# One batch of a two-level Strassen down projection taken back to one level in three of its seven products, with the weight sums made later

## The chip, the cores and the metric

The kernel runs on one core of one Trainium2 chip. The metric is device microseconds for one execution: 713.79 us is the median of three runs before the change (713.74 to 713.90). The profile is of one execution, whose own time was 713.74 us.

## The reference

Two blocks follow each other. The first is a cross attention between 512 tokens and 32 states, for 8 batches of 8 heads of 64 features, read in both directions. The second is a two-layer network with a gelu of the form h * sigmoid(1.702 h).

```
scores  = x @ state^T / 8       ; a  = exp(scores  - max) / (sum + 1e-9) ; xread = a  @ state   (512 rows per batch)
scores2 = state @ x^T / 8       ; a2 = exp(scores2 - max) / (sum + 1e-9) ; sread = a2 @ x       (32 rows per batch)
rows = [xread, sread] per batch, heads side by side -> 4352 rows of 512
h = rows @ w_in (512 x 2048) ;  g = h / (1 + exp(-1.702 h)) ;  out = g @ w_out (2048 x 512)
```

All is float32, except that the weights arrive as 64-bit floats and are rounded in the kernel.

## The kernel before, in words

**Order of the work.** The order is written out by hand: each engine executes its instructions in the order in which the program issues them, and a wait holds up all that stands behind it on that engine. TensorE works batch by batch. Batch 0 goes through a plain up projection (`up_x`) and a plain down projection (`down`, a loop over `f` = 0 to 15), during which the weights `w_out` still arrive and are rounded on VectorE, and during which batch 1's up projection runs too. From batch 1 on, each pass of the loop `for b in range(1, B)` (line 1268) is one down projection, `strassen_two` with `key` = b, followed by the up projection of batch b + 1. While the down projection of batch b runs, the attention of batch b + 1 is slipped in through *hooks*: `hooks_next` (line 901) makes a table from a place's name to a list of steps, and `hook(name)` issues them there. The 256 rows of `sread` come last.

**Strassen.** In `strassen_two` w_out has the quarters B11, B12, B21, B22, each 1024 x 256, and the gelu output has quarters of 1024 features x 256 tokens. The seven products of Strassen's method (Winograd's form) are issued as P1, P2, P5, P6, P3, P7, P4. Their right factors are B11, B21, T1 = B12 - B11, T2 = B22 - T1, B22, T3 = B22 - B12 (in the place of B12), T4 = B21 - T2. P1 and P2 are issued as *plain* products: `product` (line 742), in two halves, after each of which comes a hook (P1a, P1b and so on). Each half is 8 matmuls of 128 x 128 by 256 columns; the profile shows each of these float32 matmuls as two instructions, so 16 for a half. P5, P6, P3, P7 and P4 are issued as *low* products: `strassen_low` (line 687) uses the same method once more inside, with seven products of 4 matmuls by 128 columns (8 instructions each), small VectorE additions between them (line 701), ScalarE copies (lines 705, 711), and a hook after each (P5.1 to P5.7).

**Sums.** A low product needs three sums of blocks of its right factor (`low_sums`: three VectorE subtractions of 128 x 512, line 1210) and a fourth made in place (`low_third`). It also needs three sums and one in place of its left factor (line 752). The right factors are the same for all batches, so their sums are made once and kept in DRAM (`low_keep`, line 648). They are loaded back into two rooms `low_a` and `low_b` by `low_load` (line 645) in three parts; those of T4 go to a third room. Before the change, the sums for B22, T1, T3 and T2 are made at the end of batch 0's down loop, and those for T4 in the hook `run` of batch 1.

**Attention of the next batch, inside `strassen_two`.** The scores of batch b + 1 come at hook P2a. VectorE transposes them into `e1` (line 351) and takes maxima (lines 358, 416); ScalarE takes exponentials. The exponentials of the states' direction go out to DRAM and come back as 32 x 32 blocks (`eT_out` line 468, `eT_in` line 476), and VectorE turns each block in place (`eT_turn`, line 480). Then TensorE computes `att_sread` (line 500), which needs the turned exponentials, and two `att_M` (line 320). In every batch before the change these three stand in the hook `run`, between P3 and P7. `x_sum`, `x_inverse`, `x_scale` and `x_back` (lines 431 to 447) normalise the other direction.

**Steps the change touches.** `steps3`, `steps4` and `steps12` are the left sums for P7, P4 and P3 (four pairs of 128 x 256 each). `sums_of` and `third_of` make those of S1 (for P5) and S2 (for P6). `s4` subtracts S2 from A12 in four steps. `low4_make` makes and keeps the T4 sums in batch 1. `s12` and `s3` make S1, S2, S3. The last ones of batch 1 (line 1262) stand ahead of `strassen_two` on VectorE.

Of the kernel before, what the change touches and what calls it, by code (L numbers as in the profile page):

```python
# [10 lines left out]
FP32 = mybir.dt.float32  # L11
# [9 lines left out]
def kernel(  # L21
# [32 lines left out]
    B, H, S, D = x.shape  # L54
# [602 lines left out]
    def low4_make(a):  # L657
        t = low4_room()
        for fn, args in low_sums(T4, low_parts(t)):
            fn(*args)  # L660
        low_keep(4, t)
        a["low4"] = t

    def low4_load(a):
        a["low4"] = low4_room()
# [2 lines left out]
    def spare_M():  # L668

        m = [mpool.tile([P, NG, FC], FP32, tag=f"M{i}", name="spare_M") for i in (2, 3)]  # L670
        return [v[:, g] for v in m for g in range(NG)]
# [53 lines left out]

    def strassen_two(key, dst, hooks, a4):

        B11, B21, B22 = w_out[:, :HF, :HN], w_out[:, HF:, :HN], w_out[:, HF:, HN:]
        g = [G[key, u] for u in range(HF)]
        half = S // 2  # L730
# [45 lines left out]
        def sums_of(*pairs):  # L776
            for s, (r1, r2, r4) in pairs:
                tt(r1, whole(s, 1, 0), whole(s, 1, 1))
            for s, (r1, r2, r4) in pairs:
                tt(r2, r1, whole(s, 0, 0), ALU.subtract)  # L780
            for s, (r1, r2, r4) in pairs:
                tt(r4, whole(s, 0, 1), r2, ALU.subtract)
# [7 lines left out]

        product(bank(0), A_of(0, 0), B11, "P1")
        nc.scalar.copy(k1, bank(0))
        *r, p5 = spare_M()
        r = [v.rearrange("p (k h t) -> p k h t", k=2, h=2) for v in r]
        p5 = p5.rearrange("p (r n) -> p r n", r=2)
        sums_of((S1, r), (S2, (q1, q2, q4)))
        third_of(S1)
        product(bank(1), A_of(0, 1), B21, "P2")
        osb = opool.tile([P, 2, HN], FP32, tag="osb", name=f"osb_{key}_00")
        tt(osb, bank(1), k1)  # L800
# [6 lines left out]
        hook("P2")  # L807
        first = [lambda: s4(0), lambda: s4(1), lambda: third_of(S2), lambda: s4(2), lambda: s4(3)]
        o, h0, h1 = low_banks()

        def at(i):
            for fn in first[i - 1 : i]:
                fn()
            hook(f"P5.{i}")

        b11, t3, b21, b22 = halves_of(T1)
        strassen_low(left_of(S1, *r), (b11, t3, b21, b22, *low_b), [h0, h1, o], p5, at)
        low_load(6, 1)
        hook("P5")
        o, h0, h1 = low_banks()  # L820
        banks = [h0, o, h1]

        def sums(y, rooms):

# [31 lines left out]

        steps3, left3 = sums(y_of(0, half), (v1, v2, v4))
        steps4, left4 = sums(y_of(NU, half), (q1, q2, q4))
        steps12, left12 = sums(y_of(NU, 0), r)
        own6 = {2: steps12[:1], 5: steps12[1:2]}  # L860
        lowly("P6", left_of(S2, q1, q2, q4), T2, low_a, banks, k2, own6)
        low_load(3, 0)
        tt(k2, k2, k1)
        tt(t01, p5, k2)
        hook("P6")
        p3 = o01
        o, h0, h1 = low_banks()
        own3 = {1: steps12[2:3], 2: steps12[3:]}
        if key + 1 == B:

            own3.update({i + 3: steps3[i : i + 1] for i in range(4)})
        lowly("P3", left12, B22, low_b, [h0, h1, o], p3, own3)
        if key + 1 < B:
            low_load(5, 1)
        hook("run")
        if key + 1 < B:
            for fn in steps3:
                fn()
        hook("T")
        o, h0, h1 = low_banks()  # L880
        lowly("P7", left3, T3, low_a, [o, h0, h1], k3, {k + 1: steps4[k : k + 1] for k in range(4)})
        if key + 1 < B:
            low_load(2, 0)
        osb = opool.tile([P, 2, HN], FP32, tag="osb", name=f"osb_{key}_11")
        then = [
            lambda: tt(osb, k3, t01),
# [2 lines left out]
            lambda: tt(o01, p3, t01),  # L889
            lambda: out(0, 1, o01),  # L890
        ]
        o, h0, h1 = low_banks()
        lowly(
            "P4", left4, T4, low_parts(a4["low4"]), [o, h1, h0], k1, {2: then[:2], 3: then[2:3], 4: then[3:]}
        )
        p4 = k1
        tt(o10, p4, k3)
        out(1, 0, o10)
        free.extend(g)
# [1 line left out]
    def hooks_next(b):  # L901

        h = {}

        def at(name, fn, *args):
            h.setdefault(name, []).append((fn, args))

        at("P1a", att_state, b)
        at("P2a", att_scores, b)

        at("P2a", load_x, b)
        at("P2a", att_M, b, 0)
        at("P2a", att_M, b, 1, True)
        at("P2a", att_blocks, b)
        at("P2a", att_s_max, b)
        at("P2a", att_s_exp, b)
        at("P2a", eT_out, b)
        at("P2a", x_max, b, 0)
        at("P2a", x_sub, b, 0)
        at("P5.1", x_exp, b, 0)  # L920
        at("P5.6", att_s_norm, b)
        at("P5.6", x_max, b, 1)
        at("P5.7", x_sub, b, 1)
        at("P6.1", x_exp, b, 1)
        steps = up_sums(b)

        A[b]["sums"] = {0: steps[9:11], 1: [steps[11], steps[14]]}
        attention = [
            ("P6.1", x_sum, 0), ("P6.3", x_sum, 1), ("P6.3", x_inverse), ("P6.4", x_scale, 0),
        ]  # L930
        attention += [
            ("P6.6", x_scale, 1), ("P3.3", x_back, 0), ("P3.4", x_back, 1), ("P3.5", eT_turn, 0), ("P3.6", eT_turn, 1),
            ("P5", eT_in), ("run", att_sread), ("run", att_M, 3, True), ("run", att_M, 2),
        ]
        names = {"T": range(5), "P7.5": (5, 6), "P7.6": (7,), "P4.1": (8,), "P4.5": (12, 13)}
        for name, fn, *args in attention:
            at(name, fn, b, *args)
        for name, n in names.items():
            for i in n:
                at(name, steps[i][0], *steps[i][1])  # L940
        at("P7.2", att_srT, b)
        return h


# [264 lines left out]
    def T_of(t, x0, x1):  # L1209
        nc.vector.tensor_tensor(out=t, in0=x0, in1=x1, op=ALU.subtract)  # L1210

    def low_made(k, t, i):

        for fn, args in low_sums(t, (low_a, low_b)[i]):
            fn(*args)
        low_keep(k, turn_rooms[i])

    def low_away(k, t):

        room = apool.tile([P, NPR, S], FP32, tag="xT", name=f"away_{k}").rearrange("p j t -> p (j t)")[:, : 3 * FC]  # L1220
        for fn, args in low_sums(t, low_parts(room)):
            fn(*args)
        low_keep(k, room)


    rest = list(range(2 * nper, NF))
    for f in range(NF):
        rounds(1)
        round_to(NFC * NPR + f + 1)
        for r in range(SCH):  # L1230
            down(0, r, [f], out_x[0, r], r == SCH - 1)
        if f in (0, 2):
            for g in range(NG):
                att_eT(f // 2, g)
        if f in (0, nper * 2):
            att_M(1, 2 + f // (nper * 2))
        if f in (1, 3):
            att_sread(f // 2)
        if f in (2, 4):
            att_srT(f // 2 - 1)  # L1240
        if f % 2 == 1:
            up_x(1, rest.pop(0))
        if f == HF:
            load_state(2)
            load_x_squares(2)
        if f == NF - 2:
            T_of(T1, B12, B11)
            low_away(6, B22)
            low_made(5, T1, 1)
            for u in range(NU - 1):  # L1250
                s12(1, u, S)
            T_of(T2, B22, T1)
            low_third(T1)
        if f == NF - 1:
            for u in range(NU - 1):
                s3(1, u, S)
            T_of(B12, B22, B12)
            low_away(3, T3)
            low_third(T3)
            turn_x(2)  # L1260
            low_made(2, T2, 0)
    s12(1, NU - 1, S)
    s3(1, NU - 1, S)

# [3 lines left out]
    for b in range(1, B):  # L1268
        if b > 1:
            ahead = {"P1a": [(up_strassen(b, S, *parts_x(b), A[b]["sums"]), ())]}  # L1270
        else:
            ahead = {"P1a": [(low_third, (B22,)), (T_of, (T4, B21, T2)), (low_third, (T2,))], "P7.7": [(low_third, (T4,))]}
        if b + 1 < B:
            if b > 1:
                turn_x(b + 1)
            hooks = hooks_next(b + 1)
        else:

            steps, left, right = sr_sums()
            order = (  # L1280
                ("P5.6", 2), ("P6.1", 3), ("P6.3", 6), ("P6.4", 7), ("P7.5", 8), ("P7.6", 9), ("P4.1", 16, 17), ("P4.5", 18, 19),
            )
            hooks = {name: [steps[i] for i in n] for name, *n in order}
            hooks["P3.7"] = [(low_third, (T1,))]
            beside = steps[10:16] + [(low_third, (t,)) for t in (T2, T3, T4, B22)]
            ahead["P1a"][:0] = [steps[i] for i in (0, 1, 4, 5)]
        for name, first in ahead.items():
            hooks[name] = first + hooks.get(name, [])
        a4 = {}

        at = hooks.setdefault("run", [])
        k = 3 if b + 1 < B else 0
        at[k:k] = [(low4_load if b > 1 else low4_make, (a4,))]
        strassen_two(b, out_of(b), hooks, a4)
        if b + 2 < B:
            load_state(b + 2)
            load_x_squares(b + 2)
# [35 lines left out]
```

## Time and profile before

| what | value |
|---|---|
| median of three runs | 713.79 us |
| profiled execution, its own time / span | 713.74 / 712.0 us |
| TensorE busy | 697.9 us (98%) |
| VectorE busy | 602.0 us (85%) |
| ScalarE busy | 231.2 us (32%) |
| stretch from 154.85 to 232.04 (down of batch 1, up of batch 2) | 77.19 us |
| the five like it after it (batches 2 to 6) | 75.62 or 75.63 us each |
| granted TensorE clock, whole span | 0.998 |

A line of the timeline has the start, the length, the engine, the line of the kernel, the operation, what it writes and reads, the shapes, a count, and in brackets how long the engine was idle before it and what ended that. Matmuls overlap their successors, so the time that one takes from TensorE is read as the difference between the starts of two groups, not from the lengths.

### The profile page before, as it was taken

The page shows a single profiled execution, that of the slowest core. Times are in us where ns is not written, and L with a number is a line of the kernel's source. Part 1 is how long each engine was busy: PE and PEld are TensorE (multiplying, and loading weights), DVE is VectorE, ACT ScalarE, POOL GpSimd, SP SyncE. Part 2 cuts the span into 40 slices and gives each one's busy share as a digit, 9 for nine tenths or more (in the row PEclk, how much of TensorE's full clock was granted, in tenths as well). Part 3 has the DMA queues.
Part 4 walks back from the last instruction along what each step waited for, and adds up shares of the span by engine and source line. Part 5 has one row for each costly group of instructions (what it writes and reads, how often), then busy time and mean ns, then how long its engine had stood idle before and what let it go on. Part 6 is the DMA issues. An engine that isn't in the chain of part 4 may idle for free.

```text
span 712.0 us, 12663 instructions
## 1 busy us (share of the span) xinstructions
PE 697.9 (98%) x4973; PEld 557.9 (78%) x4975; DVE 602.0 (85%) x1246; ACT 231.2 (32%) x456; POOL 0.8 (0%) x8
## 2 busy tenths in 40 slices
PE   8989999999999999999999999999999999999996
PEld 3433444457888799888998899879987998899995
DVE  6999899969988999789968997899789997888650
ACT  5686511023214322433233322441343224300210
POOL 0000000000000000000000000000000000000000
PEclk9999999999999999999999999999999999999999
DMA  8921246217633184408550674138431940031001
GB/s 234 363 78 53 95 150 138 115 45 188 190 128 61 34 202 144 87 0 182 164 118 1 117 202 119 29 71 192 141 60 34 203 145 22 0 114 66 16 1 29
DMA packets 143770, 77.10 MB, mean 108 GB/s; under 512 B 113888, under 2 KB 127712, under 8 KB 143712
## 3 DMA queue, kind: packets, MB, share of 16 engines
q1 hardware_dynamic: 143712, 76.31, 41.1%
q8 instruction: 39, 0.64, 0.4%
q14 instruction: 19, 0.16, 0.1%
HBM read 60.29 MB, written 15.99 MB: 107 GB/s over the span
## 4 chain that ended last, share of the span: by engine, by line
PE 93%; ACT 2%; DVE 2%; DMA 2%; SPq 0%; issue 0%; DVEq 0%; ACTq 0%
PE low L696 21%; PE o L1058 17%; PE o L745 14%; PE o L696 10%; PE o L542 8%; PE h L524 7%; PE upx L1058 6%; PE M L320 4%; PE o L585 2%; PE o L320 1%; PE sr L500 1%; PE warm L125 1%; PE upx_sr L1058 1%; DMA out_dram<-osb_sr 1%; DMA xn<-in_x_dram 1%; DVE g L752 1%
## 5 line engine op out<-in xcount | busy, mean ns | idle before, releaser
L1068 DVE TENSOR_TENSOR g<-o,g 128x512 f32<-128x512 f32 (+1 forms) x140 | 88.0, 650 | 51.1 <-PE o L1058 50.2
L745 PE MATMUL o<-w_out,g 128*128 128x256 f32 x448 | 100.5, 380 | 0.0
L745 PEld LDWEIGHTS o<-w_out,g 128*128 128x128 f32 x448 | 84.2, 190 | 16.9 <-issue 5.5
L1065 ACT ACTIVATE g<-g 128x512 f32<-128x512 f32 (+1 forms) x84 | 49.8, 600 | 100.8 <-DVE g L1068 100.8
L1058 PE MATMUL upx<-aT,M 128*128 128x256 f32 x192 | 49.3, 379 | 0.0
L1058 PE MATMUL o<-ta,M 128*128 128x256 f32 x192 | 49.3, 379 | 0.0
L1058 PE MATMUL o<-ta,ms 128*128 128x256 f32 x192 | 48.3, 379 | 0.0
L696 PE MATMUL low<-low,g 128*128 128x128 f32 x336 | 44.4, 275 | 0.0
L460 ACT COPY M<-M 128x512 f32<-128x512 f32 x64 | 33.2, 596 | 28.1 <-PE M L320 28.1
L696 PEld LDWEIGHTS low<-low,g 128*128 128x128 f32 x336 | 40.9, 192 | 0.0
L1058 PEld LDWEIGHTS o<-ta,ms 128*128 128x128 f32 x192 | 36.5, 190 | 5.0
L1058 PEld LDWEIGHTS o<-ta,M 128*128 128x128 f32 x192 | 36.5, 190 | 5.0
L1058 PEld LDWEIGHTS upx<-aT,M 128*128 128x128 f32 x192 | 36.0, 190 | 4.7
L696 PE MATMUL low<-sums,later 128*128 128x128 f32 x280 | 37.1, 275 | 0.0
L696 PEld LDWEIGHTS low<-sums,later 128*128 128x128 f32 x280 | 34.6, 192 | 0.5 <-ACT pu L705 0.2
L320 PE MATMUL M<-w_in,stT 64*32 64x512 f32 x512 | 32.7, 594 | 0.2 <-ACT eT L490 0.2
L524 PE MATMUL h<-low,M 128*128 128x512 f32 x64 | 29.8, 600 | 1.4 <-DVE low L408 1.4
L696 PE MATMUL low<-w_out,g 128*128 128x128 f32 x224 | 29.7, 275 | 0.9 <-DVE pu L701 0.9
L524 PE MATMUL h<-aT,M 128*128 128x512 f32 x64 | 28.7, 599 | 1.4 <-ACT M L460 1.4
L542 PE MATMUL o<-w_out,g 128*128 128x512 f32 x64 | 28.7, 594 | 0.0
L542 PE MATMUL o<-w_out,sums 128*128 128x512 f32 x64 | 28.4, 594 | 0.0
L696 PEld LDWEIGHTS low<-w_out,g 128*128 128x128 f32 x224 | 27.3, 192 | 1.1 <-DVE pu L701 1.1
(208 smaller groups left out, 1282.2 us busy)
## 6 DMA issues: line engine op xcount, KB each, us to landing
low<-low SPq DMA_DIRECT2D x78, 256.0 KB, 3.6
later<-in_moe_w_out_dram SPq DMA_DIRECT2D x16, 512.0 KB, 3.4
xn<-in_x_dram SPq DMA_DIRECT2D x28, 256.0 KB, 4.8
low<-low SPq DMA_DIRECT2D x9, 768.0 KB, 4.6
w_out<-in_moe_w_in_dram SPq DMA_DIRECT2D x12, 512.0 KB
xsq<-in_x_dram SPq DMA_DIRECT2D x96, 64.0 KB, 2.3
out_dram<-osb SPq DMA_DIRECT2D x18, 256.0 KB, 3.0
out_dram<-later SPq DMA_DIRECT2D x14, 256.0 KB, 2.2
```

What stands on the lines that cost most here:

```text
L125: nc.tensor.matmul(ps, zeros[:, :P], zeros, start=True, stop=True)
L320: nc.tensor.matmul(ps[g][st], A[b]["stT"][rows, st], rhs(rows, j), start=True, stop=True)
L460: nc.scalar.copy(m[:, g], ps[g])
L500: nc.tensor.matmul(ps[st, g], a["eT"][:, g, c, st], xn[b][:, c, NG * j + g], start=(c == 0), stop=(c == SCH - 1),)
L524: nc.tensor.matmul(hps, lhs[i], rhs[i], start=(i == 0), stop=(i == n - 1))
L542: nc.tensor.matmul(ops, G[key, f // 2][:, f % 2, P * r : P * (r + 1)], w_out[:, f], start=(f == 0), stop=(f == NF - 1))
L585: nc.tensor.matmul(ps[:, r], lhs[f][:, P * r : P * (r + 1)], rhs[:, f], start=(first and r == 0 and f == 0), stop=(f == HF - 1), skip_grou ...
L696: nc.tensor.matmul(ps, lhs[f], rhs[:, f], start=(first and f == 0), stop=(f == QF - 1), skip_group_check=True)
L745: nc.tensor.matmul(ps[:, r], lhs[f][:, P * r : P * (r + 1)], rhs[:, f], start=(r == 0 and f == 0), stop=(f == HF - 1), skip_group_check=True,)
L1058: nc.tensor.matmul(ps[:, k], lhs[i][:, o : o + P], rhs[i], start=(first and k == 0 and i == 0), stop=(i == n - 1), skip_group_check=True,)
L1065: nc.scalar.activation(out=dst, in_=src, func=AF.Gelu_apprx_sigmoid)
L1068: nc.vector.tensor_tensor(out=dst, in0=ps, in1=x, op=ALU.add)
```

## The change

In batch 1 alone (`plain`, where `a4` is None), P5, P3 and P4 are issued as plain products, and P6 and P7 stay low. The left sums for P5, P3 and P4 are not made there. The sums of the right factors T2, T3, T1 and B22 are no longer made at the end of batch 0's down loop but during batch 1: T2 in P1a, T3 in P1b, B22 in P7.4 to P7.6 and T1 in P4.7, and they are kept in DRAM from there. P6 and P7 of batch 1 use the rooms as they were just filled, and the loads of batch 1 go, except one. The in-place sum of T4 moves from P7.7 of batch 1 to P3.6 of batch 2. The attention of batch 2 is issued at other places: its maxima together in P2a, its normalising between P6.1 and the end of P6, the turning of its exponentials after P6, and `att_sread`, the two `att_M` and the T4 sums after the first half of P3. Batches 2 to 7 are otherwise issued as before. The transport of the states' exponentials by 32 x 32 blocks (`eT_out`, `eT_in`) and the reload in three parts (`low_load`) are the same in both kernels.

```diff
@@ low4_make
-        a["low4"] = t
@@ strassen_two
+        plain = a4 is None
...
-        *r, p5 = spare_M()
...
-        sums_of((S1, r), (S2, (q1, q2, q4)))
-        third_of(S1)
+        if plain:
+            sums_of((S2, (q1, q2, q4)))
+        else:
...
+        if plain:
+            for fn in first:
                 fn()
-            hook(f"P5.{i}")
...
+            p5 = bank(0)
+            product(p5, [S1[:, f, :half] for f in range(HF)], T1, "P5")
+            hook("P5")
+            banks = [h0, h1, o]
...
-        own6 = {2: steps12[:1], 5: steps12[1:2]}
+        own6 = {}
...
         tt(k2, k2, k1)
         tt(t01, p5, k2)
+        if plain:
+            for fn in steps3:
+                fn()
+            hook("P6")
+            p3 = bank(3)
+            product(p3, A_of(0, 1), B22, "P3")
+            o, h0, h1 = low_banks()
+            lowly("P7", left3, T3, low_b, [h0, h1, o], k3, {})
...
+        else:
+            for fn in then:
+                fn()
+            product(bank(2), A_of(1, 1), T4, "P4")
+            for i in range(1, 8):
+                hook(f"P4.{i}")
+            p4 = bank(2)
@@ hooks_next
+        if b > 2:
...
+        else:
+            at("P2a", x_max, b, 1)
+            at("P2a", x_sub, b, 1)
+            at("P2a", x_exp, b)
+            at("P2", att_s_norm, b)
...
+        else:
+            attention += [("P6.5", x_scale, 1), ("P6.6", x_back, 0), ("P6", x_back, 1), ("P6", eT_turn, 0), ("P6", eT_turn, 1)]
+            names = {"P3a": range(7), "P7.1": (7,), "P7.2": (8,), "P7.3": (12, 13)}
+            run, turned = "P3a", "P3b"
+        attention += [("P5", eT_in), (run, att_sread), (run, att_M, 3, True), (run, att_M, 2)]
@@ end of batch 0's down loop
             T_of(T1, B12, B11)
-            low_away(6, B22)
-            low_made(5, T1, 1)
...
             T_of(T2, B22, T1)
-            low_third(T1)
...
             T_of(B12, B22, B12)
-            low_away(3, T3)
-            low_third(T3)
             turn_x(2)
-            low_made(2, T2, 0)
@@ for b in range(1, B)
+            if b == 2:
+                ahead["P3.6"] = [(low_third, (T4,))]
         else:
-            ahead = {"P1a": [(low_third, (B22,)), (T_of, (T4, B21, T2)), (low_third, (T2,))], "P7.7": [(low_third, (T4,))]}
+            ahead = {
+                "P1a": low_sums(T2, low_a)
+                + [(low_keep, (2, turn_rooms[0])), (T_of, (T4, B21, T2)), (low_third, (T2,))],
+                "P1b": low_sums(T3, low_b) + [(low_keep, (3, turn_rooms[1])), (low_third, (T3,))],
+                "P4.7": low_sums(T1, low_b) + [(low_keep, (5, turn_rooms[1])), (low_third, (T1,)), (low_third, (B22,))],
+            }
+            for k, step in zip((4, 5, 6), low_sums(B22, low_a)):
+                ahead[f"P7.{k}"] = [step]
+            ahead["P7.6"] += [(low_keep, (6, turn_rooms[0])), (low_load, (2, 0))]
...
-        at = hooks.setdefault("run", [])
+        at = hooks.setdefault("run" if b > 1 else "P3a", [])
...
-        strassen_two(b, out_of(b), hooks, a4)
+        strassen_two(b, out_of(b), hooks, a4 if b > 1 else None)
```

## The prediction

> **What bounds the kernel now.** I read the page's busy line and the shares of the chain first, then the busy time of each engine by stage, then the timeline of TensorE and of VectorE through batch 1, and last the queue's.
>
> ```profile
> PE 697.9 (98%) x4973; PEld 557.9 (78%) x4975; DVE 602.0 (85%) x1246; ACT 231.2 (32%) x456; POOL 0.8 (0%) x8
> PE 93%; ACT 2%; DVE 2%; DMA 2%; SPq 0%; issue 0%; DVEq 0%; ACTq 0%
> ```
>
> TensorE sets the end. A microsecond added to its stream is a microsecond of time, and one taken off VectorE is worth nothing unless TensorE waited for it.
>
> ```profile
> 154.85:232.04 77.19, 75.25 (x596) 66.23 (x595) 65.09 (x136) 25.11 (x51) 0.00 (x0) 1.00 0.51 138
> 232.04:307.66 75.62, 75.62 (x603) 67.30 (x603) 66.41 (x140) 25.23 (x51) 0.00 (x0) 1.00 0.47 110
> ```
>
> The columns are the stretch, its length, busy us of PE, PEld, DVE, ACT and POOL, then clock, DMA share and GB/s. Batch 1 has 2 us of open TensorE waits; batch 2 has none. The TensorE timeline shows the price of both kinds of product, and where batch 1 loses:
>
> ```profile
> 154.69 3.62 PE L745 MATMUL o<-w_out,g 128*128 128x256 f32 x16
> ...
> 171.55 1.05 PE L696 MATMUL low<-sums,later 128*128 128x128 f32 x8
> 172.44 1.06 PE L696 MATMUL low<-low,spare_M 128*128 128x128 f32 x8
> ...
> 191.37 1.10 PE L500 MATMUL sr<-xn,eT 128*32 128x64 f32 x64
> 192.40 1.95 PE L320 MATMUL M<-w_in,stT 64*32 64x512 f32 x32
> 194.27 1.16 PE L696 MATMUL o<-w_out,g 128*128 128x128 f32 x8
> ...
> 197.75 1.06 PE L696 MATMUL low<-low,later 128*128 128x128 f32 x8
> 199.75 1.16 PE L696 MATMUL low<-w_out,g 128*128 128x128 f32 x8 [0.94 <-DVE pu L701]
> ```
>
> Low groups of 8 start 0.893 us apart, so a low product is 7 x 0.893 = 6.25. In the chain a run of 16 of line 745 takes 3.45, so a plain product is 6.91. By starts, batch 1 now runs P5 from 171.55 for 7.10, P6 for 6.30, P3 for 6.42, the hook `run` for 2.90, P7 for 8.90, P4 for 6.26, to 209.43: together 37.88. Without waits it would be 5 x 6.25 + 2.90 + 0.11 (one transpose in P7) = 34.26. So 3.62 us are lost, 2.54 of them in P7, where VectorE is late after making the T4 sums.
>
> ```profile
> 132.34 0.68 DVE L1210 TENSOR_TENSOR away<-w_out 128x512 f32<-128x512 f32 x1
> 133.06 1.42 DVE L1210 TENSOR_TENSOR away<-w_out,away 128x512 f32<-128x512 f32 x2
> 134.39 0.68 DVE L1210 TENSOR_TENSOR low<-sums 128x512 f32<-128x512 f32 x1
> ...
> 159.93 0.69 DVE L565 TENSOR_TENSOR later<-g,g 128x512 f32<-128x512 f32 x1 [3.62 <-ACT g L527]
> 160.66 0.69 DVE L566 TENSOR_TENSOR later<-later,g 128x512 f32<-128x512 f32 x1
> 161.27 0.68 DVE L571 TENSOR_TENSOR g<-g 128x512 f32<-128x512 f32 x1
> ...
> 190.04 0.69 DVE L480 STREAM_TRANSPOSE eT<-eT 128x512 f32<-128x512 f32 x1
> 190.66 0.25 DVE L701 TENSOR_TENSOR later<-o,pu 128x128 f32<-128x128 f32 x1
> 190.84 0.69 DVE L480 STREAM_TRANSPOSE eT<-eT 128x512 f32<-128x512 f32 x1
> ```
>
> From 159.93 to 191.5 VectorE works without a pause, and the second turn of the exponentials ends just as `att_sread` (191.37) comes to need it. That is the tight place.
>
> **Removed from batch 0's end.** Twelve sums and two in-place sums are 4 x 2.05 + 1.2 = 9.4 us of VectorE (a set of three takes from 132.34 to 134.39). Gain: 0. TensorE has no wait there, and VectorE's next step, at 159.93, waits for ScalarE's last gelu, which stands behind four output copies 2.7 us apart (150.60 to 158.81), each waiting for the output DMA before it. These stay, so VectorE has nothing to start early: the freed time becomes idle time, and the work comes back after 161.87.
>
> **TensorE's own price.** Three plain for three low products: 3 x (6.91 - 6.25) = +1.96 us. Rule against row: the Trainium skill, TensorE: Matmul & The Clock Gate, Back-to-back issue gap, gives about 81 ns per matmul at 128 columns and 131 at 512 in a sustained stream with weight loads. By it (an estimate, 98 ns at 256 columns between them) a plain product would be 3.1 us and a low one 4.5, and the three exchanges -4.2 us. The rows are 216 and 112 ns per instruction, nearly in proportion to the columns, and I take them.
>
> **VectorE through batch 1.** The sum is made from 161.87, when `s3` has issued; each term is a distance between starts in the rows of before.
> - P1a and P1b: T2's sums 2.05, T4 2.31 (162.47 to 164.78), in-place sum 0.62, T3's sums 2.05, in-place sum 0.60. To 169.50. Before, this place held 3.53, to 165.40.
> - Sums of S2 alone: 2.05, to 171.55 (before 4.21 for both and the in-place one).
> - Block transposes 1.23, state maxima 1.54, two pairs of maximum and subtraction 2.64: to 176.96. Output add 0.60, norms 0.51, the four `s4` and one in-place sum 3.12: to 181.19.
>
> TensorE meanwhile: P2 ends at 171.55 as before. P5 needs only S1, T1 and bank 0, all ready: to 178.46. P6's first four groups go to 182.03. VectorE's first addition there comes after one `x_sum` (0.60), so it ends about 182.1 and the fifth group starts at 182.15. Then `x_sum` and inverse 1.20, addition: done 183.45, so the sixth group waits from 183.04 to 183.50. P6 ends at 185.28: +0.57 of waits.
> - After P6 on VectorE: last addition to 185.96 (it waits for the product), `k2` 0.73, `t01` 0.61, `steps3` 2.69 (194.59 to 197.28), `x_back` 0.62. The first turn starts at 190.6 and ends at 191.3; the second ends at 191.9.
> - TensorE needs only P3's first half, 3.45, in that time: it is at `att_sread` at 188.74 and waits 2.6 us. This is the new wait. Behind it on TensorE's queue stand both `att_M`, P3's second half, P7 and P4; nothing passes.
> - `att_sread` with its second half waiting for the second turn: to 192.5. `att_M` twice 1.87: 194.37. P3's second half 3.45, transpose 0.11: 197.93. The T4 sums (2.05), four `ta` (1.5) and one `ms` (0.6) on VectorE end near 196.7, now beside P3's second half: P7's 2.54 loss goes. P7 has 5.3 us of VectorE work in 6.25: no wait. P7 to 204.18, P4 to 211.09. T1's sums and two in-place sums (3.2) lie beside P4 on VectorE.
>
> Against 209.43 batch 1 ends 1.66 later. As a sum: +1.96 - 3.62 + 0.57 + 2.6 + 0.15 = +1.66. Bounds: if P6 did not wait at all, its last addition would end at 185.2 and the rest of the chain is the same, which gives +0.9. Upward, the nearest row is the largest single TensorE wait for VectorE now, 197.75 to 199.75 less 0.89 = 1.1: +2.8. I take +1.66, because most of the wait (6.2 us of VectorE against 3.45 of TensorE after P6) holds whenever VectorE arrives.
>
> **The clock.** The rows have 1.00 in every stage, but none holds a TensorE wait as long as 2.6 us in this part. The same page, Part 1, lets the clock fall to half after about 3.4 us of idle; by it 2.6 us keeps the clock, and if the window were crossed, 3.4 us at half clock would add about 1.7 (an estimate). No run here shows it; the sum has 0 for it.
>
> **Queues.** The kept sums of T2 and T3 now leave at about 163.9 and 168.9, and the loads of x stand behind them on SP: from about 169.2 (now 166.63), needed at 188.7. `eT_out` waits for ScalarE, 175.4 instead of 173.30; the rows
>
> ```profile
> 173.30 3.13 SPq L468 DMA_DIRECT2D squares<-e x4
> ...
> 180.71 2.57 SPq L476 DMA_DIRECT2D eT<-squares x4
> ```
>
> with 3.0 us to landing put the way there and back at 13 us: about 188.4, 2.2 ahead of the first turn. Three reloads less compete with it. Cost 0; past 190.6 each microsecond counts.
>
> **Batch 2.** One in-place sum (0.62) now stands before the second turn. Now that turn runs from 268.89 to 269.58, and `att_sread` starts at 269.42, its second half near 269.95. With the sum the turn ends at 270.2: +0.3, bounds 0 and 0.6. It is idle time of VectorE later (0.97 at 280.85) that absorbs the rest. Batches 3 to 7 are unchanged.
>
> Sum: 713.74 (this execution; 0.05 under the median) + 1.66 + 0.3 = **715.7**.
>
> **Rivals.** 0.2% (1.43 us: 712.36 and 715.22) is about what a measurement of this kernel can tell from no change.
> - *The turned exponentials are in time.* Then -3.62 + 1.96 = -1.66 remains, with P6's 0.57 and batch 2's 0.3 or without: 712.1 to 713.0, faster at its lower end, not slower anywhere. Its place is the start of `att_sread`, its price the 2.6 + 0.15 us there; from about 0.8 us of wait downwards the change is no loss. For it: the present order fits to 0.2 us. Against it: six VectorE steps are written between P6 and the turn. 0.07.
> - *P6 runs free, the wait is shorter:* 714.6 to 715.0, within. For it: the waits in P6 are 0.1 and 0.46, small differences of long sums. 0.20.
> - *The exponentials land late or VectorE lags more:* 716.8 to 717.3. For it: the DMA engines are about nine tenths busy from 173 to 186. Against it: three loads go. 0.13.
> - The forecast itself, 715.2 to 716.6: 0.60.
> - That the change does nothing: excluded, since 3 x 0.65 us of matmuls are added and VectorE's order differs.
>
> **How the numbers follow.** 715.7 is the likeliest. The range 714.5 to 717.1 runs from +0.9 with nothing in batch 2 to +2.8 with 0.6. Slower: 0.13 and most of the 0.60 make 0.68. Within: 0.20, a little of the forecast, and the slower half of the first rival, 0.27. Faster: 0.05.
>
> **What would show it.** Right: a wait of 2 to 3 us before line 500 in batch 1, put down to line 480; P7 of batch 1 in about 6.4 us instead of 8.9; batch 1's waits in P7 gone; batches 3 to 7 at 75.62. Wrong: line 500 starting within 0.5 us of P3's first half, a wait put down to `eT_in`, a clock under 1.00 after the wait, or a plain product off 6.9.

## The result, and the profile after

The changed kernel takes 717.82 us (median; 716.14 to 717.89) against 713.85 us: a ratio of 1.0049 with a 95% interval of 1.0032 to 1.0067. It is slower, as forecast, but by 4.0 us and not by 1.96, and 717.82 lies above the range that ended at 717.1. The profiled execution took 717.80 us, its span is 716.0 us.

The page of the changed kernel, busy line and chain:

```profile
PE 700.4 (98%) x4901; PEld 556.8 (78%) x4903; DVE 591.4 (83%) x1211; ACT 229.8 (32%) x449; POOL 0.8 (0%) x8
PE 87%; DVE 5%; DMA 3%; ACT 2%; issue 1%; SPq 1%; DVEq 0%; ACTq 0%
```

VectorE has 10.6 us less to do than before (602.0), and yet 5% of the chain now runs through it, against 2% before. The stages, with the columns as in the prediction (stretch, length, busy us of PE, PEld, DVE, ACT, POOL, clock, DMA share, GB/s):

```profile
154.84:235.68 80.84, 78.19 (x524) 65.30 (x523) 61.86 (x112) 23.61 (x44) 0.00 (x0) 0.98 0.46 122
235.68:311.67 75.99, 75.83 (x603) 67.35 (x603) 66.92 (x141) 25.22 (x51) 0.00 (x0) 1.00 0.46 109
311.67:387.30 75.63, 75.63 (x604) 67.31 (x603) 66.41 (x140) 25.23 (x51) 0.00 (x0) 1.00 0.46 110
```

All of the loss is in two stages: batch 1 takes 80.84 us instead of 77.19 (+3.65), batch 2 75.99 instead of 75.62 (+0.37). From batch 3 on nothing has changed. The new thing in the first line is the clock, 0.98. TensorE's timeline through batch 1 of the changed kernel:

```profile
171.54 7.07 PE L746 MATMUL o<-sums,later 128*128 128x256 f32 x32
178.44 1.05 PE L695 MATMUL low<-sums,later 128*128 128x128 f32 x8
...
185.53 3.62 PE L746 MATMUL o<-w_out,g 128*128 128x256 f32 x16
191.49 1.25 PE L500 MATMUL sr<-xn,eT 128*32 128x64 f32 x64 [2.34 <-DVE eT L480]
192.67 3.64 PE L320 MATMUL M<-w_in,stT 64*32 64x512 f32 x32
196.24 3.72 PE L746 MATMUL o<-w_out,g 128*128 128x256 f32 x16
199.80 0.27 PE L514 MATMUL srT<-ident,sr 128*128 128x128 f32 x1
199.91 1.06 PE L695 MATMUL low<-w_out,g 128*128 128x128 f32 x8
...
206.16 7.07 PE L746 MATMUL o<-sums,g 128*128 128x256 f32 x32
213.07 1.03 PE L1100 MATMUL upx<-aT,M 128*128 128x256 f32 x4
```

Read from the starts, P5 takes 6.90 us and P4 6.91 as plain products, P6 takes 7.09, and P7 takes 6.25 (8.90 before). `att_sread` waits 2.34 us for the turned exponentials. And the two `att_M` behind it, which took 1.87 us before (192.40 to 194.27), take 3.57. What happened to them stands in the clock of short stretches (the third column from the right) of the same execution:

```profile
189.00:191.40 2.40, 0.15 (x1) 0.00 (x0) 2.40 (x7) 0.00 (x0) 0.00 (x0) 1.00 0.00 0
191.40:192.60 1.20, 1.11 (x64) 0.98 (x64) 0.63 (x2) 0.00 (x0) 0.00 (x0) 1.00 0.00 0
192.60:194.40 1.80, 1.80 (x36) 0.56 (x31) 1.52 (x3) 0.52 (x2) 0.00 (x0) 0.55 0.03 9
194.40:196.20 1.80, 1.80 (x24) 0.17 (x8) 1.77 (x5) 1.07 (x2) 0.00 (x0) 0.50 0.26 106
196.20:198.00 1.80, 1.80 (x16) 1.58 (x9) 0.76 (x2) 1.07 (x2) 0.00 (x0) 1.00 0.82 331
```

TensorE stands still from about 189.1 to 191.5, runs `att_sread` at full clock, and then gets half the clock for 3.4 us, in which the `att_M` happen to lie. VectorE's side of the wait:

```profile
186.85 0.69 DVE L753 TENSOR_TENSOR later<-o,later 128x512 f32<-128x512 f32 x1
187.46 0.75 DVE L753 TENSOR_TENSOR later<-g,g 128x256 f32<-128x256 f32 x2
188.13 0.75 DVE L753 TENSOR_TENSOR later<-later,g 128x256 f32<-128x256 f32 x2
188.80 0.75 DVE L753 TENSOR_TENSOR g<-g 128x256 f32<-128x256 f32 x2
189.47 0.75 DVE L753 TENSOR_TENSOR later<-g,later 128x256 f32<-128x256 f32 x2
190.15 0.70 DVE L447 STREAM_TRANSPOSE aT<-e 128x512 f32<-128x512 f32 x1
190.77 1.26 DVE L480 STREAM_TRANSPOSE eT<-eT 128x512 f32<-128x512 f32 x2
```

The four pairs from 187.46 are `steps3`; then one `x_back`, then the two turns, the first at 190.77.

### The profile page after: what moved, and what is told of

It is laid out like the page before. It is cut to its first block, busy times and chain, and to the rows that moved or that the text cites. A ratio compares the mean times of both kernels' runs of the same rounds, so it can differ in the third digit from the quotient of the medians.

```text
span 716.0 us, 12443 instructions
## 1 busy us (share of the span) xinstructions
PE 700.4 (98%) x4901; PEld 556.8 (78%) x4903; DVE 591.4 (83%) x1211; ACT 229.8 (32%) x449; POOL 0.8 (0%) x8
## 4 chain that ended last, share of the span: by engine, by line
PE 87%; DVE 5%; DMA 3%; ACT 2%; issue 1%; SPq 1%; DVEq 0%; ACTq 0%
PE low L695 17%; PE o L1100 17%; PE o L746 13%; PE o L695 8%; PE o L542 7%; PE h L524 7%; PE upx L1100 6%; PE M L320 4%; PE o L585 2%; DMA xn<-in_x_dram 2%; PE o L320 1%; PE sr L500 1%; PE warm L125 1%; PE upx_sr L1100 1%; DMA out_dram<-osb_sr 1%; DMA out_dram<-osb 1%
## 5 line engine op out<-in xcount | busy, mean ns | idle before, releaser
L746 PE MATMUL o<-w_out,g 128*128 128x256 f32 x480 | 107.9, 381 | 0.0
L746 PEld LDWEIGHTS o<-w_out,g 128*128 128x128 f32 x480 | 90.1, 190 | 19.2 <-issue 7.2
L695 PE MATMUL low<-low,g 128*128 128x128 f32 x304 | 40.2, 275 | 0.0
L695 PEld LDWEIGHTS low<-low,g 128*128 128x128 f32 x304 | 37.0, 192 | 0.0
L695 PE MATMUL low<-sums,later 128*128 128x128 f32 x264 | 35.0, 275 | 0.1
L320 PE MATMUL M<-w_in,stT 64*32 64x512 f32 x512 | 34.4, 622 | 0.2 <-ACT eT L490 0.2
L695 PEld LDWEIGHTS low<-sums,later 128*128 128x128 f32 x264 | 32.7, 192 | 0.7 <-DVE pu L700 0.3
L565 DVE TENSOR_TENSOR later<-g,g 128x512 f32<-128x512 f32 (+1 forms) x32 | 20.8, 650 | 14.6 <-ACT g L527 14.6
```

The lines of the kernel that those rows point to most:

```text
L320: nc.tensor.matmul(ps[g][st], A[b]["stT"][rows, st], rhs(rows, j), start=True, stop=True)
L565: nc.vector.tensor_tensor(out=s1, in0=a21, in1=a22, op=ALU.add)
L695: nc.tensor.matmul(ps, lhs[f], rhs[:, f], start=(first and f == 0), stop=(f == QF - 1), skip_group_check=True)
L746: nc.tensor.matmul(ps[:, r], lhs[f][:, P * r : P * (r + 1)], rhs[:, f], start=(r == 0 and f == 0), stop=(f == HF - 1), skip_group_check=True,)
```

## The experiments

The theory after the result: the plain products, VectorE's lateness and the wait went as worked out, and the wait cost once more, through the clock. The rivals: the `att_M` are slow for another reason, or the clock's fall belongs to something else in the change. All comparisons are with runs of the kernel before on the same chip, 713.91 to 713.96 us in the median.

**The wait filled.** Ten matmuls of the identity, whose result is not read, are put into the wait.

```diff
+    def fill_wait():
+        for _ in range(10):
+            nc.tensor.matmul(bank_o[2][:, :P], ident, ident, start=True, stop=True)
...
+        if b == 2:
+            at("P3a", fill_wait)
         attention += [("P5", eT_in), (run, att_sread), (run, att_M, 3, True), (run, att_M, 2)]
```

> The changed kernel with ten matmuls of the identity, 128 x 128 by 128 columns, issued just ahead of att_sread in batch 1; their result is never read. They add 2.2 us of TensorE work inside the wait of 2.34 us, so the data path is the same. Theory (the clock fell because TensorE sat idle there): granted clock 1.00 through batch 1, the two att_M together 1.88 us instead of 3.57, every run at about 716.1 us. Rival (the att_M were slow for another reason, such as their PSUM copies on ScalarE or the loads): they stay at 3.57 and the time at 717.8 us.

Measured: 716.23 us, five runs from 716.19 to 716.40; ratio 1.0033 (1.0020 to 1.0046). The timeline of this kernel:

```profile
188.97 2.39 PE L935 MATMUL o<-ident 128*128 128x128 f32 x20
191.47 1.25 PE L500 MATMUL sr<-xn,eT 128*32 128x64 f32 x64
192.65 1.95 PE L320 MATMUL M<-w_in,stT 64*32 64x512 f32 x32
194.53 3.72 PE L746 MATMUL o<-w_out,g 128*128 128x256 f32 x16
```

and its clock where the changed kernel had 0.50:

```profile
194.40:196.20 1.80, 1.80 (x16) 1.50 (x9) 1.77 (x5) 1.48 (x4) 0.00 (x0) 1.00 0.27 109
```

`att_sread` starts at the same time to 0.02 us, the `att_M` take 1.88 us, and 1.6 us of the loss are gone. Their data, their PSUM copies and the DMA traffic (109 GB/s in the last stretch, 106 before) are the same here, so it was the idle TensorE ahead of them that made the `att_M` slow. None of the five runs lies near 717.8; of the changed kernel itself six of nine do, with the next runs counted in.

**The changed kernel once more**, unchanged, for the runs' spread.

> The changed kernel itself, unchanged, for how often its clock falls. Theory (whether a wait of 2.3 us makes the clock fall depends on where it lies in a grid of fixed windows that does not start with the kernel): two kinds of runs, at about 716.15 and 717.85 us with nothing between, most of them the slower kind, as in the first three of four. Rival (the one run at 716.14 was an outlier of another origin): all at 717.85.

Measured: 716.19, 716.44, 717.62, 717.67 and 717.96 us. With the four of the result, three of nine runs lie at 716.14 to 716.44 and six at 717.62 to 717.96, none between. The profiled execution of this label is one of the first kind, with the same wait as in the result:

```profile
191.81 1.25 PE L500 MATMUL sr<-xn,eT 128*32 128x64 f32 x64 [2.34 <-DVE eT L480]
192.99 1.95 PE L320 MATMUL M<-w_in,stT 64*32 64x512 f32 x32
194.86 3.72 PE L746 MATMUL o<-w_out,g 128*128 128x256 f32 x16
```

So the same wait lets the clock fall in some executions and not in others. The traces show why. They keep the times at which the granted clock changes, and in each of the twelve profiles of this case these times lie whole multiples of 3.413 us apart; the first comes between 4.1 and 6.9 us after the start. In the profile of the result they are 5.05, 192.78, 196.19 and 715.02 us, which is 0, 55, 56 and 208 steps. So the clock changes only at the ends of a grid of windows, and the grid does not start with the kernel. What goes with a fall is how long TensorE was busy in the window before. The table has the window with the most of the wait in it; labels that begin with x3 and x7 are experiments further down, and "changed" is the profile of the result.

| profile | window (us) | TensorE busy in it | clock in the next window |
|---|---|---|---|
| changed | 189.37 to 192.78 | 1.29 of 3.41 | 0.50 |
| `x3_late4` | 191.97 to 195.38 | 1.38 | 0.50 |
| `x7_dense_after` | 190.19 to 193.61 | 1.46 | 0.50 |
| `x0_again` | 187.78 to 191.20 | 1.69 | 1.00 |
| `x3_late2` | 191.22 to 194.63 | 2.10 | 1.00 |
| `x3_late3` | 189.25 to 192.66 | 2.17 | 1.00 |

In `x0_again` the end of a window (191.20) cuts the wait in two, 1.73 us before it and 0.61 after. In every window of the twelve profiles, from the first change on, the same holds: after 1.46 us of busy time or less the clock is at half, after 1.69 or more it is full. The six upper times are not all of one height (717.62 to 717.96), which was not expected and stays open.

**The turns ahead of `steps3`.**

```diff
         if plain:
+            hook("P6")
             for fn in steps3:
                 fn()
-            hook("P6")
             p3 = bank(3)
```

> The changed kernel with the two turns of the exponentials issued ahead of steps3 (2.69 us of VectorE) instead of behind it. Theory (the wait is the VectorE work between P6 and the turns, and the clock follows from the wait): the first turn ends at about 188.8 us instead of 191.5, TensorE arrives at 189.0 and waits 0 to 0.4 us, the clock stays at 1.00, batch 1 ends near 208.7 instead of 213.1, the time is about 713.4 us. Rival (the exponentials themselves come back late from DRAM): the wait stays above 1.5 us and is put down to a DMA, 716 us or more.

Measured: 713.72 us, ten runs from 713.66 to 713.81; ratio 0.9998 (0.9988 to 1.0007), no difference from before. The timeline:

```profile
185.58 3.62 PE L746 MATMUL o<-w_out,g 128*128 128x256 f32 x16
189.13 1.10 PE L500 MATMUL sr<-xn,eT 128*32 128x64 f32 x64
190.16 1.95 PE L320 MATMUL M<-w_in,stT 64*32 64x512 f32 x32
```

Moving 2.7 us of VectorE work from one side of three instructions to the other is worth 4.1 us of the result's median. The exponentials were back from DRAM in time. The rest of the change, with this wait taken out, is worth nothing in either direction. Of the 3.62 us that batch 1 lost before, the plain products take 1.96, P6's waits 0.86 (178.47 to 185.58, against 6.25), two delays in P3 0.2 and batch 2 0.37. The prediction's first rival had priced this very case at 712.1 to 713.0.

**The sum of T4 taken out of batch 2**, on top of that.

```diff
-            if b == 2:
-                ahead["P3.6"] = [(low_third, (T4,))]
...
-                "P4.7": low_sums(T1, low_b) + [(low_keep, (5, turn_rooms[1])), (low_third, (T1,)), (low_third, (B22,))],
+                "P4.7": low_sums(T1, low_b) + [(low_keep, (5, turn_rooms[1])), (low_third, (T1,)), (low_third, (B22,)), (low_third, (T4,))],
```

> The changed kernel with the turns ahead of steps3 (as in x2_turn_first) and with the in-place sum of T4 moved from P3.6 of batch 2 to the end of P4 of batch 1. Theory (that one VectorE instruction ahead of the second turn is why batch 2 takes 75.99 us instead of 75.62): batch 2 at 75.62, 713.35 us, 0.37 under x2_turn_first. Rival (batch 2 is longer for what batch 1 leaves behind): 75.99 again, 713.7 us.

Measured: 713.37 us (ten runs, 713.22 to 713.47), 0.35 under `x2_turn_first`, and batch 2 of this kernel:

```profile
231.24:306.87 75.63, 75.63 (x604) 67.31 (x602) 66.43 (x140) 25.21 (x51) 0.00 (x0) 1.00 0.48 110
```

One instruction of 0.62 us ahead of the second turn was the 0.37 us of batch 2.

**The wait alone, in the kernel before.** The plain products might have their own part in the clock's fall. So the wait is made in the kernel before: n VectorE instructions that change nothing (the maximum of a tile with itself) are put ahead of both turns in P3.6 of batch 1, n = 4, 3 and 2.

```diff
+    def delay(b, n):
+        for k in range(n):
+            t = A[b]["e1"][:, k % 2]
+            nc.vector.tensor_tensor(out=t, in0=t, in1=t, op=ALU.max)
...
-            ("P6.6", x_scale, 1), ("P3.3", x_back, 0), ("P3.4", x_back, 1), ("P3.5", eT_turn, 0), ("P3.6", eT_turn, 1),
+            ("P6.6", x_scale, 1), ("P3.3", x_back, 0), ("P3.4", x_back, 1), ("P3.6" if b == 2 else "P3.5", eT_turn, 0), ("P3.6", eT_turn, 1),
...
+        if b == 2:
+            at("P3.6", delay, b, 4)
```

> The kernel before, with four VectorE instructions of 128 x 512 that change nothing put ahead of the two turns in P3.6 of batch 1 (and the first turn moved there from P3.5). All products stay low. Theory (any wait of some 2.4 us at att_sread costs itself and lets the clock fall): a wait of 2 to 2.6 us there, 716.2 us in runs where the clock holds, and 1.7 us more, 717.9, in runs where it falls to half for 3.4 us. Rival (the fall belongs to the plain products or to the changed order): 716.2 us in all runs, clock 1.00.

> x3_late4 with three VectorE instructions instead of four: the wait at att_sread is about 1.9 us, between the 1.31 that left the clock alone in ten runs and the 2.52 at which it fell. Theory (a grid of windows 3.4 us long, and a window must be idle for more than half): the clock holds in most or all runs, 715.9 to 716.1 us. Rival (anything much over 1.31 lets it fall): a mean clock that is lower by 0.001 to 0.002 in most runs, and times in two groups.

> x3_late4 with two idle-handed VectorE instructions instead of four: the wait at att_sread is 1.2 to 1.4 us. Theory (a short wait costs its own length and leaves the clock alone): 715.1 us in all runs. Rival (any wait over a microsecond there lets the clock fall): 1.00 is lost in some runs and these are 0.5 us or more above the others.

| n | wait at `att_sread` | median us (range, runs) | `att_M` twice, in the profile |
|---|---|---|---|
| 2 | 1.31 | 715.47 (715.34 to 715.87, 10) | 1.88 |
| 3 | 1.91 | 715.99 (715.89 to 716.39, 6) | 1.88 |
| 4 | 2.52 | 716.99 (716.80 to 717.60, 4) | 3.47 |

The timeline for n = 4:

```profile
194.00 1.25 PE L500 MATMUL sr<-xn,eT 128*32 128x64 f32 x64 [2.52 <-DVE eT L480]
195.18 3.54 PE L320 MATMUL M<-w_in,stT 64*32 64x512 f32 x32
198.65 1.22 PE L696 MATMUL o<-w_out,g 128*128 128x128 f32 x8
...
205.96 1.06 PE L696 MATMUL o<-sums,g 128*128 128x128 f32 x8
```

The clock falls in a kernel that has no plain product in P5, P3 and P4, so the fall belongs to the wait. The forecast 717.9 for such runs was too high, and 715.1 for n = 2 was 0.4 too low. After the fall P7 takes 7.31 us (198.65 to 205.96); with n = 3 and no fall it takes 8.90 as before. VectorE catches up while TensorE is slow, its 0.94 us wait in P7 is gone, and so 1.6 us come back. Of the four runs with n = 4, the profiled one took 716.81 us with a fall, and one took 716.80 with a mean clock of 0.998, too high for a fall inside the kernel.

The mean clock tells that because the clock is also at half at the very end, for 0.6 to 3.8 us in the twelve profiles; a fall adds 3.4, and a mean of 0.998 leaves at most 3.6 in all. All ten runs with n = 2 have 0.998 or more, so none had a fall. With n = 3 the profile has none, but there the end of a window (192.66) cuts the wait into 1.23 and 0.68 us, so it does not show what 1.91 us in one window do. One of the six runs, 716.39 us at 0.996, was at half clock for 5.0 us or more and so had a fall. No length of the wait is a limit by itself; it counts how much of it lies in one window.

**Another order behind the wait.** `att_sread` is narrow (32 of 128 columns of weights, 64 columns of data). If its 1.2 us count as idle, the idle stretch would be 3.5 us. So the `att_M`, with 512 columns of data, are put ahead of it, behind two small matmuls that need the turned exponentials.

```diff
+    def touch_eT(b):
+        eT = A[b]["eT"]
+        for g in range(NG):
+            nc.tensor.matmul(bank_o[2][:, :P], eT[:, g, 0], ident, start=True, stop=True)
...
+        attention += [(run, att_sread), (run, att_M, 3, True), (run, att_M, 2)] if b > 2 else [
+            (run, touch_eT), (run, att_M, 3, True), (run, att_M, 2), (run, att_sread)]
...
-        k = 3 if b + 1 < B else 0
+        k = (4 if b == 1 else 3) if b + 1 < B else 0
```

> The changed kernel with another order behind the wait: two matmuls of 128 columns that need the turned exponentials stand first, then the two att_M (1.88 us of full matmuls), then att_sread. The wait of TensorE is as long as before (2.3 us). Theory (idle time of that length is enough to let the clock fall): it falls to half in most runs, 717.6 to 717.9 us. Rival (the 1.2 us of narrow matmuls of att_sread behind the wait count as idle too, and only both together make the clock fall): it holds in all runs, 716.1 us.

Measured: 717.98, 718.20, 719.29 and 719.58 us. The profile has the clock at half although `att_sread` no longer stands behind the wait:

```profile
192.00:194.00 2.00, 1.85 (x20) 0.94 (x28) 0.58 (x1) 0.00 (x0) 0.00 (x0) 0.90 0.00 0
194.00:196.00 2.00, 2.00 (x24) 0.27 (x8) 0.00 (x0) 1.07 (x2) 0.00 (x0) 0.50 0.00 0
```

A wait of 2.34 us is enough in this order too, here in two of four runs by times and mean clock (0.995 and 0.996, the others 0.998). For the rival this alone does not decide, since the `att_M`, called full in the expectation, have narrow weights as well (64 x 32). `x0_again` does: its window from 191.20 to 194.61 has 0.61 us of the wait and then nothing but these narrow matmuls, 2.80 us busy in all, and the clock stays full. So they count as work. The forecast of the time missed by over a microsecond: in this order `att_sread` waits 0.68 us for ScalarE's copies of `att_M`, and the profiled execution was already 0.56 us later at the end of P6.

**What the kernel before loses in batch 1.** Two kernels look for its 3.62 us. The first moves T4 and two in-place sums, 3.5 us of VectorE, to where VectorE waits for ScalarE at the end of batch 0.

```diff
             low_made(2, T2, 0)
+            low_third(B22)
+            T_of(T4, B21, T2)
+            low_third(T2)
     s12(1, NU - 1, S)
...
-            ahead = {"P1a": [(low_third, (B22,)), (T_of, (T4, B21, T2)), (low_third, (T2,))], "P7.7": [(low_third, (T4,))]}
+            ahead = {"P7.7": [(low_third, (T4,))]}
```

> The kernel before, with T4 and the in-place sums of B22 and T2 (3.5 us of VectorE) moved from P1a of batch 1 to just ahead of the last s12 of batch 1, where VectorE has 3.6 us of idle time. Theory (VectorE was late through batch 1 of the kernel before, 3.62 us of lost TensorE time): batch 1 loses about 1 us instead of 3.62, 711.2 us. Rival (the losses have other causes, as ScalarE's copies): within 0.5 us of 713.8.

Measured: 713.04 us (ten runs, 712.96 to 713.13); ratio 0.9988 (0.9978 to 0.9997). P5 now takes 6.25 us instead of 7.10, but P7 still 8.91 (193.52 to 202.43). The expectation was wrong: the sums in P1a are worth 0.85 us, and P7's loss does not come from them. The second adds one part of the change: P4 of batch 1 plain, without its left sums, with the T4 sums beside it (and the in-place sum of T4 in P4.7).

```diff
-        lowly("P7", left3, T3, low_a, [o, h0, h1], k3, {k + 1: steps4[k : k + 1] for k in range(4)})
+        lowly("P7", left3, T3, low_a, [o, h0, h1], k3, {k + 1: steps4[k : k + 1] for k in range(4)} if key > 1 else {})
...
+        else:
+            for fn in then:
+                fn()
+            p4 = bank(2)
+            product(p4, A_of(1, 1), T4, "P4")
+            for i in range(1, 8):
+                hook(f"P4.{i}")
...
-        at = hooks.setdefault("run", [])
+        at = hooks.setdefault("run" if b > 1 else "P4.6", [])
```

> The kernel x6_hoist with one part of the change on top: P4 of batch 1 as a plain product, without its left sums, and the T4 sums (2.05 us of VectorE) made beside it instead of ahead of P7. Theory (P7's 2.54 us of lost time come from the T4 sums and the left sums for P4; a plain product costs 0.65): P7 of batch 1 in about 6.4 us instead of 8.9, P4 in 6.9 instead of 6.26, 711.2 us. Rival (VectorE is late in P7 for other work): P7 above 8 us, 713.5 us.

Measured: 711.27 us, four runs from 711.25 to 711.31; ratio 0.9962 (0.9947 to 0.9977): faster than both kernels. Its timeline, with P7 from 193.51 to 199.97 and P4 behind it, and its batch 1, in which TensorE never waits:

```profile
193.51 1.16 PE L696 MATMUL o<-w_out,g 128*128 128x128 f32 x8
...
199.97 7.07 PE L745 MATMUL o<-sums,g 128*128 128x256 f32 x32
```

```profile
155.00:229.33 74.33, 74.33 (x571) 65.42 (x570) 62.01 (x123) 24.48 (x49) 0.00 (x0) 1.00 0.54 142
```

The plain product costs 0.66 us, and with it 2.45 us of waiting in P7 go (8.91 to 6.46). How much of that belongs to the T4 sums and how much to the left sums for P4 was not separated.

## Why the prediction was right and wrong

- *Right: the price of the plain products.* Forecast 6.91 each; P5 took 6.90 and P4 6.91. The rate read from the rows held. The rule of the Trainium skill (TensorE: Matmul & The Clock Gate, Back-to-back issue gap) that would have made plain products cheaper than low ones does not describe these float32 matmuls: P5's 32 instructions follow each other after 216 ns.
- *Right: the wait, its place and its size.* Forecast: TensorE at `att_sread` at 188.74, a wait of 2.6 us, the first turn started at 190.6. Measured: P3's first half over at 188.98, the turn at 190.77, `att_sread` at 191.49. `x2_turn_first` shows that `steps3` ahead of the turns makes the wait.
- *Right: P7's loss goes* (6.25 us), nothing is gained at batch 0's end, and the exponentials are back in time.
- *A little short: P6's waits* were 0.84 us instead of 0.57, `att_sread` came 0.15 later, P3's second half took 3.56 instead of 3.45, and batch 2 cost 0.37 instead of 0.3.
- *Wrong: "the sum has 0 for it", the clock.* This is the step that failed. In the profiled execution it cost 1.70 us (3.57 us for the `att_M` instead of 1.87). Batch 1 ends 3.64 us later than before (213.07 against 209.43): the 1.66 of the forecast, 0.17 by the end of `att_sread`, 1.70 for the clock and 0.11 in P3's second half. The prediction had the price right as an unlikely extra, had even named a clock under 1.00 after the wait as a sign of being wrong, and set it to 0 because the Trainium skill (TensorE: Matmul & The Clock Gate, Part 1) asks for about 3.4 us of idle. The runs decide against that reading: a wait of 2.34 us was enough in six of nine runs of this kernel, and a window with 1.46 us of work in it was still followed by half the clock. The kernel before was not at 1.00 in every stage either: from 685.55 on it has 0.95, with the clock at half from 709.59, after the last matmul. Where the clock held, the time was 716.14 to 716.44, inside the range and 0.4 to 0.7 above the forecast.
- *The range* had no case for the clock at all, although the text gave its price. With 1.7 us on top of 715.7 as a case it would have reached 717.4 and with the bounds of the others beyond 717.9. Two smaller readings slipped as well: P6 without its waits takes 0.57 off the +1.66, which makes +1.09 and not +0.9, and the DMA engines were 0.78 busy from 173 to 186, not nine tenths (0.92 only from 177 to 182).

## What to carry to other kernels

When a change puts a wait into TensorE's stream, price the wait twice: its own length, and, if it can leave TensorE busy for less than about half of a window of 3.4 us, half-speed matmuls in the next window (here 1.46 us of work in a window were too little and 1.69 enough). Where the wait lies in the grid changes from run to run, so waits of about 1.9 to 2.5 us gave two kinds of runs. If the wait cannot be removed, work that nobody reads may be cheaper than an idle TensorE (here 1.6 us). On an engine with a written order, the first question for a new wait is which instructions stand ahead of the needed one without being needed as soon: here four pairs of additions ahead of two transposes were the loss, as `x2_turn_first` is no slower than the kernel before.

## What was not expected of the hardware

- The granted clock went to 0.50 for 3413 ns each time that a profile shows it inside the kernel, in three kernels. It began not in the wait but at the end of a window, 1.3 to 1.6 us after work had resumed (in the changed kernel at 192.78, against 191.49).
- Less than 3.4 us of idle is enough: a wait of 1.31 us never showed a fall in ten runs, 1.91 us showed one in one of six, 2.34 us in six of nine.
- A slower TensorE can give time back: with n = 4, 1.6 us of VectorE's lateness in P7 disappeared behind the half-speed matmuls.
